# The inverse table of a long convolution: one transposing DMA in place of sixteen TensorE transposes, with a new order of all work

## The chip, the cores and the metric

One Trainium2 chip, of which the kernel uses one core. The metric is the device time in microseconds (us) of one execution. The engines are named as the profile names them: PE (matmuls on TensorE, with PEld its weight loads), ACT (ScalarE), DVE (VectorE), POOL (GpSimd) and SP (the engine that issues most DMAs; DMAs that ACT and POOL issue are named so).

## The reference, cut to what matters

The inputs are 2048 tokens of 640 channels in bf16. The token-wise part is a normalisation and a gated feed-forward network with 1728 hidden units; the sequence part is a causal convolution over all 2048 tokens for each channel, written with FFTs of length 4096.

```python
x = A_q
xn = _layernorm(x, axis=-1)
s = _A_ref(xn, A_k, A_v, A_shift_k, A_ssm_k, A_ssm_D)
g = _silu(_B_ref(xn, B_w1, B_b1, B_w2, B_b2))
return x + s * g
# _A_ref: k_shift = a causal filter of 4 taps over k;  kv = k_shift * v
#         y = irfft(rfft(kv, 4096) * rfft(ssm_k, 4096))[:2048] + kv * ssm_D;  returns xn * y
# _B_ref: h = gelu(x @ w1 + b1);  returns h @ w2 + b2
```

## The kernel before

**Tiles.** The tokens are cut into 16 tiles of 128 rows, tile `i` holding tokens 32k+16h+i (k is 0 to 63, h is 0 or 1). Everything stays in SBUF but the convolution's intermediate results, which pass through three scratch tensors in HBM to be laid out anew.

**The convolution.** The transform is done in two steps on PE. Step 1 multiplies each tile with a table `W` (128 x 16 x 128, one 128 x 128 block for each tile): operations `K1_i`, `K1r_Q` for the filter and `U1_i`, `U1r_Q` for the signal, evicted from PSUM by `Ke`, `Ker`, `Ue`, `Uer` and stored by `Ks_Q`, `Us_Q`. Step 2 loads a slice s of 8 (`KL_s`, `UL_s`) and multiplies with a small table (`K2_s_r`, `U2_s_r`, and `X2_s` for the last 128 channels of both), evicted by `Kf`, `Uf`. The products are `pr_s_w` and `pq_s_w` on DVE. The inverse goes the same way: `i1_s` and `i1r` (evicted by `ie`, `ir`), stores `cs_s`, loads `cl_r`, and `i2_i`, whose weights are `G`, the inverse table. `G` is `W` with each 128 x 128 block transposed, and nothing but `i2` reads it. `ym_i` multiplies the result by the gated and normalised tile, `ad_i` adds x, `os_i` stores.

**The tables.** The angles of `W` are integers made in three groups of tiles (0 to 3, 4 to 9, 10 to 15): `wm` (a multiplication and an addition, on DVE or POOL), `wq` (a mask, on DVE) and `ws` (two sines on ACT).

**The feed-forward part.** `bn_i` takes statistics, `rs_g` (POOL) the reciprocal deviations of a group of tiles, `xn_i` normalises, `xt_i` transposes on PE and `xe_i` evicts. `f1_c_r_ft` is the first matmul for a chunk c of four tiles and 128 hidden units (in two halves r of 256 tokens for chunk 0 and ft below 5, otherwise 512 tokens at once), `ge` its gelu on ACT. `f1h`, `geh` are the last 64 units. `f2_i_h` is the second matmul, 14 products for a half of 320 channels, or 28 of 64 columns each where the order marks it `/N`; `si_i` is the silu on ACT and `gx_i` multiplies on DVE. A change between sine, gelu and silu on ACT loads a table (line 686).

**The shift filter and kv** are the `kv` operations on DVE. `wu_j` are groups of four warm-up matmuls on a zero tile.

**The order.** The functions only declare operations with what they read and write. The string `ORDER` lists all of them, and `Plan.emit` issues them in exactly that order, each on its engine: so every engine's program, and each DMA queue, is a subsequence of `ORDER`. A token `name/E@slots` carries a choice of engine (`A` for ACT, `D` for DVE, `G` for POOL, `S` for SP, `N` for the split matmul; without a letter the first that the operation allows, which is ACT for evictions) and the buffers that it takes from pools: for PE operations a bank of PSUM, of which there are 8 (`@6`, or 6 and 7 for an operation that takes two). A bank can be written again when the operation that evicts it is done. Waits between engines follow from the data.

The inverse table is made in the lines above `w2l`: two PSUM banks are filled with eight transposes each (`gt0`, `gt1`, line 503), and each is copied to `G` by one eviction (`gte0`, `gte1`, line 181, the line of all evictions). In the order before they stand between the first `xt`, and the copies go to DVE.

Of the kernel before, what the change touches and what calls it, by code (L numbers as in the profile page):

```python
# [55 lines left out]
class Plan:  # L56
# [6 lines left out]
    def op(self, name, eng, fn, reads=(), writes=(), hold=(), func=None):  # L63
        o = Op()
        o.name, o.engs, o.fn, o.func = name, eng.split("|"), fn, func
        o.reads, o.writes = list(reads), list(writes)
# [8 lines left out]
        return o
# [39 lines left out]
def h3_block(ctx: ExitStack, tc: tile.TileContext, x_d, k_d, v_d, sk_d, K_d, D_d, w1_d, b1_d, w2_d, out_d):  # L115
    nc = tc.nc
# [63 lines left out]
    def evict(e, out_, in_):  # L180
        (nc.scalar.copy if e == "ACT" else nc.vector.tensor_copy)(out=out_, in_=in_)  # L181

    ps = Pool(8, lambda k, sz: ps_t[:, k:k + 2, :] if sz == 2 else ps_t[:, k, :])
# [310 lines left out]
                out=xn_t[:, i, a:b], in0=xn_t[:, i, a:b], in1=s_.v[:, a:b], op=ALU.mult),  # L494
               reads=[slh[n]], writes=[xnb[i][n]], hold=[s_])

    for g in range(2):
        pb = Buf(pool=ps)

        def gt(e, g=g, pb=pb):  # L500
            o = pb.v.bitcast(BF16).rearrange("p (a b) -> p a b", b=P)
            for t in range(8):
                nc.tensor.transpose(out=o[:, t, :], in_=W_t[:, 8 * g + t, :], identity=ident[:])
# [195 lines left out]
K1_7@6 Ker_1/A f1_0_0_9@4 xl4 Kl0 xn4 Dl/A kl1 f1_0_1_4@5 xn5 Ke_7/A Kl3 xn7 f1_0_0_10@0 xn6 ge_0_0_9 kv0_0@0 Ks_1  # L699
xt5@1.1 ge_0_1_4 f1_0_0_1@2 xe5/A xt4@3 kv0_1m@1 xt7@6 xt6@7 xe7/A f1_0_0_11@4 xe6/A kv0_1a f1_0_0_4@5 xe4/A  # L700
f1_0_1_3@1 ge_0_0_10 f1_1_0_5@6.1 ge_0_0_1 kv0_2m@1 ge_0_0_4 ge_0_1_3 K1_14@2 ge_1_0_5 K1r_3@0 kv0_2a f1h_1@7 Ke_14/A
f1_0_0_12/N@5 Ker_3/A bn12 f1_1_0_9/N@6 ge_0_0_11 Ks_3 bn13 vl0 ge_0_0_12 f1_1_0_8/N@2 w2l1 ge_1_0_9 vl1 kv0_3m@1 w2l0
geh_1 f1h_0@3 ge_1_0_8 K1_8@0.2 K1_10@4 kv0_3a K1_9@6 geh_0 f1_1_0_11@2 Ke_8/A bn14 f1_1_0_0@3 Ke_10/A bn15 f1_1_0_2@0
# [10 lines left out]
kv3_2a U1_15@0.0 U1_14@6 Ue_15/A f2_2_1 kv3_3m@1 Ue_14/A kv3_3a kv3_4 f1_3_0_7@4.0 si_2 bn9 U1_12@0 U1_13@6 Ue_12/A
U1r_3@2 Ue_13/D f1_3_0_4@5 Uer_3/A bn11 K2_2_0@0 K2_3_0@6 Us_3 f1_3_0_5@2 bn10 f1_3_0_12@3 ge_3_0_4 Kf_2_0/D rs3
ge_3_0_7 f1_3_0_0@5 ge_3_0_5 ge_3_0_12 xn8 xn11 K2_7_0@0 ge_3_0_0 xt8@4.0 f1_3_0_9@2 Kf_3_0/A xe8/D xn9 K2_2_1@4 UL0@6
ge_3_0_9 xt11@3 Kf_2_1/D UL1@3 xt9@6 Kf_7_0/A UL2@8 f1_3_0_3@7 UL6@9 xe11/D UL3@10 xe9/D KL6@7 K2_0_1@4 ge_3_0_3
K2_1_1@0 xn10 K2_3_1@2 Kf_0_1/A xt10@6 Kf_3_1/D f1_3_0_1@7 Kf_1_1/A gx_2 K2_7_1@4 xe10/D X2_0@2 ge_3_0_1 gx_5 U2_0_0@0
# [62 lines left out]
```

## Time and profile before

| | |
|---|---|
| median of 3 runs | 183.62 us (183.51 to 183.87) |
| profiled execution, its own time | 184.05 us |
| its span, from first to last instruction | 182.3 us |
| granted TensorE clock | 1.0 |
| busy: PE, DVE, ACT, POOL | 175.0, 160.9, 138.5, 22.6 us |

The profile's views used below: a page with busy times and the costliest groups of instructions (line, engine, operation, result and sources, count, then busy time and mean duration in ns); stretches of the span with the busy time of each engine and the number of its instructions in brackets; the chain of work that ended last (start, duration, engine, result, line, count); and the timeline (start, duration, engine, line, operation, count, and in brackets the idle time before it and what ended it). PEq, SPq and the like are the engines' sequencers, which issue DMAs.

### The profile page before, as it was taken

How to read it: one execution, taken by the hardware profiler on the slowest of the kernel's cores; microseconds unless marked ns; L12 is line 12 of the kernel's file. 1: busy time of each engine (PE TensorE's matmuls, PEld its weight loads, DVE VectorE, ACT ScalarE, POOL GpSimd, SP SyncE). 2: the span in 40 equal slices, each digit the busy share in tenths (PEclk: the TensorE clock that was granted, in tenths of full speed). 3: DMA queues.
4: the chain of work that ended last, by engine and by line, in shares of the span. 5: the costliest groups of instructions: out<-in, count | busy, mean ns of one | idle time of the engine just before them, and what ended most of it. 6: DMA issues, size and time to landing. Idle time of an engine off the chain costs nothing.

```text
span 182.3 us, 5182 instructions
## 1 busy us (share of the span) xinstructions
PE 175.0 (96%) x2192; PEld 99.9 (55%) x2192; DVE 160.9 (88%) x252; ACT 138.5 (76%) x201; POOL 22.6 (12%) x52
## 2 busy tenths in 40 slices
...
GB/s 187 411 415 403 199 367 407 334 425 432 409 309 403 417 358 397 153 287 76 222 340 367 172 141 158 148 325 377 148 4 88 206 287 132 416 405 392 66 189 144
DMA packets 19417, 50.64 MB, mean 278 GB/s; under 512 B 1729, under 2 KB 13506, under 8 KB 17986
## 3 DMA queue, kind: packets, MB, share of 16 engines
...
q8 instruction: 17, 0.28, 0.6%
...
HBM read 31.95 MB, written 18.35 MB: 276 GB/s over the span
## 4 chain that ended last, share of the span: by engine, by line
PE 81%; DVE 8%; ACT 7%; issue 1%; ACTq 0%; DVEq 0%
PE ps L435 30%; PE ps L476 30%; PE ps L349 4%; PE ps L604 4%; PE ps L563 4%; PE ps L413 3%; PE ps L664 2%; DVE xn L668 2%; ACT v L181 2%; DVE stats L381 2%; ACT L686 1%; ACT k L181 1%; PE ps L360 1%; PE ps L450 1%; DVE w L238 1%
## 5 line engine op out<-in xcount | busy, mean ns | idle before, releaser
L476 PE MATMUL ps<-w,hT 128*64 128x320 bf16 (+4 forms) x644 | 65.0, 293 | 0.0
L435 PE MATMUL ps<-xnT,w 128*128 128x512 bf16 (+2 forms) x300 | 61.2, 362 | 0.5 <-ACT sl L489 0.2
L476 PEld LDWEIGHTS <-hT 128*64 128x64 bf16 (+3 forms) x644 | 45.3, 105 | 17.4 <-issue 3.9
L435 PEld LDWEIGHTS <-w 128*128 128x128 bf16 (+1 forms) x300 | 26.4, 99 | 28.5 <-issue 6.2
L181 ACT CAST st<-ps 128x1024 bf16<-128x1024 f32 x36 | 35.0, 1014 | 3.4 <-PE ps L360 1.8
L439 ACT ACTIVATE hT<-ps,b1f 128x512 bf16<-128x512 f32 (+1 forms) x57 | 35.0, 665 | 1.2 <-PE ps L435 1.0
L489 ACT ACTIVATE sl<-ps 128x640 bf16<-128x640 f32 (+2 forms) x18 | 11.6, 647 | 24.0 <-PE ps L476 19.4
L529 DVE TENSOR_TENSOR lat<-lat 128x2560 bf16<-128x2560 bf16 (+1 forms) x15 | 18.4, 1225 | 0.5
L526 DVE TENSOR_TENSOR lat<-k,lat 128x2560 bf16<-128x2560 bf16 (+1 forms) x15 | 18.3, 1218 | 0.2
L181 ACT CAST k<-ps 128x1024 bf16<-128x1024 f32 (+2 forms) x19 | 16.2, 878 | 2.6 <-PE ps L563 1.5
L181 ACT CAST v<-ps 128x1024 bf16<-128x1024 f32 (+2 forms) x18 | 14.5, 839 | 0.4 <-PE ps L563 0.4
L668 DVE TENSOR_TENSOR xn<-ps,xn 128x640 bf16<-128x640 f32 x16 | 12.6, 819 | 2.2 <-PE ps L664 2.0
L493 DVE TENSOR_TENSOR xn<-xn,sl 128x640 bf16<-128x640 bf16 (+2 forms) x18 | 8.0, 448 | 7.3 <-ACT sl L489 7.2
L181 DVE CAST k<-ps 128x1024 bf16<-128x1024 f32 (+2 forms) x14 | 11.8, 857 | 2.3 <-PE ps L563 0.9
L381 DVE BATCH_NORM_STATS2 stats<-x 128x6 f32<-128x320 bf16 x32 | 13.7, 470 | 0.0
L686 ACT ACT_TABLE_LOAD x8 | 10.3, 1283 | 0.1
L396 POOL TENSOR_SCALAR rstd<-mv 128x4 f32<-128x4 f32 (+1 forms) x5 | 1.3, 257 | 69.2 <-DVE mv L382 69.2
L181 ACT CAST lat<-ps 128x1024 bf16<-128x1024 f32 (+2 forms) x12 | 9.4, 826 | 0.2 <-PE ps L604 0.2
L604 PE MATMUL ps<-st,I 32*64 32x512 bf16 x256 | 8.8, 380 | 0.1
L332 PE MATMUL ps<-hT 128*128 128x512 bf16 x24 | 7.5, 477 | 1.2 <-DVE mhalf L212 1.2
L181 DVE CAST lat<-ps 128x1024 bf16<-128x1024 f32 (+2 forms) x9 | 7.9, 892 | 0.7 <-PE ps L604 0.3
L181 ACT COPY xnT<-ps 128x640 bf16<-128x640 bf16 x8 | 5.3, 695 | 3.9 <-PE ps L413 3.9
...
## 6 DMA issues: line engine op xcount, KB each, us to landing
...
v<-in_v SPq DMA_DIRECT2D x4, 640.0 KB, 7.6
k<-scrK SPq DMA_DIRECT2D x4, 640.0 KB, 7.4
v<-scrK SPq DMA_DIRECT2D x4, 640.0 KB, 9.9
w<-in_w SPq DMA_DIRECT2D x2, 1120.0 KB, 10.3
x<-in_x SPq DMA_DIRECT2D x3, 640.0 KB, 6.8
k<-in_k SPq DMA_DIRECT2D x3, 640.0 KB, 7.2
```

The lines of the kernel that those rows point to most:

```text
L181: (nc.scalar.copy if e == "ACT" else nc.vector.tensor_copy)(out=out_, in_=in_)
L381: nc.vector.bn_stats(out=stats[:, i, h, :], in_=x_t[:, i, h * H:(h + 1) * H])
L435: nc.tensor.matmul(out=pb.v[us, 0:b - a], lhsT=w1_t[:, ft, t, us], rhs=xnTb[c].v[:, a // P:b // P, t, :], start=(t == 0), stop=(t == DT - 1))
L439: nc.scalar.activation(out=hTb[c].v[:, ft, a:b], in_=pb.v[:, 0:b - a], func=ACT.Gelu_apprx_tanh, bias=b1_f[:, ft:ft + 1], scale=1.0)
L476: nc.tensor.matmul(out=o[us, 0:b - a], lhsT=hTb[c].v[0:M, ft, q * P + us.start:q * P + us.stop], rhs=w2_t[0:M, ft, a:b], start=(ft == 0), ...
L489: nc.scalar.activation(out=o_, in_=i_, func=ACT.Silu)
L493: op("gx_" + nm, "DVE", lambda e, a=a, b=b: nc.vector.tensor_tensor(out=xn_t[:, i, a:b], in0=xn_t[:, i, a:b], in1=s_.v[:, a:b], op=ALU.mul ...
L526: op("kv%d_%dm" % (r, j), "DVE", lambda e, i=i, n=n, j=j, t=t, wb=wb: nc.vector.tensor_tensor(out=t.v[:, 0:n, :], in0=k_t[:, i + 3 - j:i + ...
L529: op("kv%d_%da" % (r, j), "DVE", lambda e, n=n, t=t, a=a: nc.vector.tensor_tensor(out=a.v[:, 0:n, :], in0=a.v[:, 0:n, :], in1=t.v[:, 0:n, ...
L604: nc.tensor.matmul(out=pb[j // 2].v[64 * a:64 * a + 64, j % 2, :], lhsT=I1_t[32 * j:32 * j + 32, m, :], rhs=o[w][32 * j:32 * j + 32, a, r, ...
L668: op("ym_%d" % i, "DVE", lambda e, i=i, pb=pb: nc.vector.tensor_tensor(out=xn_t[:, i, :], in0=pb.v.rearrange("p a b -> p (a b)")[:, 0:D], ...
L686: nc.scalar.activation(out=tab[:], in_=cst[:], func=func)
```

## The change

The sixteen transposes `gt` and the two evictions `gte` are taken out. One operation `gT` on SP takes their place, a DMA that reads `W` from SBUF and writes `G` in SBUF, transposing each block. It needs all of `W`, and `i2` needs it, as before. All other functions are as they were. The string `ORDER` is replaced as a whole: nearly every operation has another place, many have other PSUM banks, and some go to another engine (`wm0` from DVE to POOL, `sx`, a scaling of a small table, from DVE to POOL, `b1c` from POOL to DVE; 11 of the 16 `xe` on ACT in place of 8, 13 of the 16 `ir` on ACT in place of 9; 14 of the 33 `f2` with `/N` in place of 13). `gT` stands in SP's queue behind the loads `UL0` and `UL1` and ahead of `UL6` and `UL3`; `UL2` goes from SP to POOL.

```diff
-    for g in range(2):
-        pb = Buf(pool=ps)
-
-        def gt(e, g=g, pb=pb):
-            o = pb.v.bitcast(BF16).rearrange("p (a b) -> p a b", b=P)
-            for t in range(8):
-                nc.tensor.transpose(out=o[:, t, :], in_=W_t[:, 8 * g + t, :], identity=ident[:])
-
-        op("gt%d" % g, "PE", gt, reads=Wb + [idb], writes=[pb])
-        op("gte%d" % g, "ACT|DVE", lambda e, g=g, pb=pb: evict(
-            e, G_t[:, 8 * g:8 * g + 8, :], pb.v.bitcast(BF16).rearrange("p (a b) -> p a b", b=P)), reads=[pb], writes=[Gb[g]])
+    op("gT", "SP", lambda e: nc.sync.dma_start_transpose(
+        out=G_t[:], in_=W_t[:].rearrange("p i b -> p (i b)")), reads=Wb, writes=Gb)
...
-b1l/A grid xl1 zz c0 xl0 wu2@0 fix wm0 wm2/G Kl4 w1l0 wm1 xl2 w1l2 wu4@1 wq0 Kl1 wq1 w1l1 sm0 Kl2 wq2 wu0@2 bn2 ws2 id
-skl bn3 ws1 wu5@3 bn1 rs1 w1l3 K1_12@4.0 K1_13@6 K1_15@0 bn0 kl0 Ke_13/A wu3@2 ws0 xn2 wu1@3 rs0 xn3 Ke_12/A xt2@6.0
-gt1@7 b1c xe2/D xt3@2 xn1 gt0@3 xe3/A xn0 xt1@6 sm1 xt0@4 xe1/A f1_0_1_1@5.0 xe0/D sm2 f1_0_1_0@2 bn4 f1_0_0_7@6
-gte0/D ge_0_1_1 f1_0_0_8@4 bn5 ge_0_1_0 ge_0_0_7 Ke_15/A f1_0_1_2@5 bn7 f1_0_0_5@3 ge_0_1_2 gte1/D ge_0_0_8 one1 bn6
-K1_4@0.2 ge_0_0_5 K1_5@6 f1_0_0_0@2 Ke_4/A Ke_5/D rs2 f1_0_0_6@5 ge_0_0_0 sm3 K1_6@0 ge_0_0_6 K1r_1@2 one0 Ke_6/D
...
-pr_7_1@1 i1r_3@0.4 Uf_5_1/A f2_11_1 ir_6_0/A pr_5_0@3 ir_7_0/A ir_7_1/D i1_7@2.0 ir_6_1/D si_11 pr_5_1@2 cs_6/S
-f1_3_0_10@4 ie_7_1/A ie_7_0/D i1_5@6.0 cs_7/S f2_10_0@2.1 ie_5_0/A ie_5_1/D gx_11 cs_5/S f2_10_1 f1h_3@5 si_10
-f2_8_1/N@6.0 cl_0@8 gx_10 cl_2@6 cl_1/G@10 cl_5/G@4 f2_8_0/N cl_7/G@7 cl_3/G@0 f2_9_0/N@0.1 cl_6/G@1 si_8 gx_8 i2_1@2
-i2_0@6 ge_3_0_10 ym_1 f2_9_1/N geh_3 ad_1 ym_0 i2_5@2 ad_0 i2_4@4 ym_5 f2_14_1/N@6.0 si_9 os_0 os_1 ym_4 cl_4@2 ad_4
-i2_3@0 gx_9 os_4 i2_2@2 ym_3 i2_10@4 f2_14_0/N ym_10 ym_2 i2_11@0 ad_2 si_14 i2_14@4 ym_11 f2_12_1/N@2.1 os_2 ym_14
...
+b1l/A grid xl1 zz xl0 wu5@0 fix wm1 wm2/G w1l0 Kl4 w1l1 wq1 xl2 wu1@1 c0 ws1 w1l2 Kl2 id wq2 w1l3 bn3 wm0/G ws2 wu2@2
+skl bn2 kl0 wu3@3 bn0 rs1 wu4@4 bn1 Kl3 K1_13@6.0 K1_15@0 xn2 Ke_13/A K1_12@2 rs0 xn3 xt2@5.0 xt3@4 xe2/D Ke_15/A
+wu0@6 sm0 xn1 xn0 xe3/A xt1@7 wq0 xt0@5 b1c/D f1_0_1_0@6.0 xe1/D xe0/A Ke_12/D f1_0_1_4@0 ws0 f1_0_1_2@1 sm1
+f1_0_0_8@4 bn5 sm2 f1_0_0_6@7 ge_0_1_0 bn7 ge_0_1_4 f1_0_0_4@5 ge_0_0_6 bn4 f1_0_0_3@2 ge_0_0_4 f1_0_0_5@3 ge_0_1_2
+bn6 ge_0_0_3 ge_0_0_8 K1r_1@6.2 ge_0_0_5 K1_7@0 K1_4@4 rs2 f1_0_0_7@2 Ker_1/D Ke_4/A K1_6@4 ge_0_0_7 one0 K1_5@6 xn4
...
+Kf_3_0/A f1_3_0_7@4 ge_3_0_0 xn8 f1_3_0_4@5 ge_3_0_7 xn11 xn10 xn9 UL0@3 K2_3_1@0 ge_3_0_4 K2_1_1@2 UL1@8 UL2/G@9
+K2_2_0@6 Kf_1_1/A gT f1_3_0_1@4 Kf_2_0/D sx Kf_3_1/A xt8@5.1 xt9@2 xe8/D xt11@3 ge_3_0_1 K2_2_1@6 xe11/D K2_0_1@0
...
+Kf_7_2/D Uf_7_2/D f2_11_0@2.1 ie_4_1/A pq_7_1 pq_7_0 ie_4_0/A pr_7_1@2 i1r_3@0.6 cs_4/S pr_7_0@0 U2_5_1@4 ir_7_1/A
+f2_11_1 ir_6_0/A ir_6_1/A Uf_5_1/D ir_7_0/A cs_6/S pr_5_0@1 i1_7@6.0 si_11 pr_5_1@3 f1_3_0_10@4 ie_7_0/A gx_11
+ie_7_1/A i1_5@2.6 gx_4 cs_7/S f2_8_0@0.1 ie_5_0/D ie_5_1/A cs_5/S f1h_3@5 f2_8_1/N geh_3 f2_10_0/N@6.0 si_8 cl_0@9
+cl_2@8 cl_5/G@7 gx_8 cl_1/G@4 f2_10_1/N cl_6/G@6 cl_7/G@0 f2_9_0/N@2.1 si_10 cl_3/G@1 gx_10 i2_0@0 i2_1@6 ge_3_0_10
+ym_0 f2_9_1/N ym_1 ad_0 ad_1 i2_5@4 si_9 i2_4@0 ym_5 f2_14_1/N@6.0 ad_5 ym_4 os_5 os_1 i2_10@2 ad_4 cl_4@3 i2_3@4 gx_9
+i2_2@0 os_4/A f2_14_0/N ym_2 ym_10 ym_3 i2_11@0 si_14 f2_12_1/N@2.1 ad_3 ad_2 os_3/A ym_11 ad_10 i2_12@4 i2_14@6 ym_12
...
```

More of the change, by code (lines that the diff above doesn't have):

```diff
@@ L699 @@
[L699 to L703, printed above, removed]
@@ L714 @@
[L714 to L718, printed above, removed]
@@ new lines @@
+ge_0_0_0 f1h_1@1.1 ge_0_0_9 f1h_0@0 kv0_2m@1 geh_1 f1_1_0_2/N@6 geh_0 kv0_2a f1_1_0_8/N@7 ge_1_0_2 ge_0_0_1 K1_14@2
+K1_10@0.2 kv0_3m@1 Ke_14/A K1r_3@4 f1_1_0_5@6 Ker_3/A bn12 f1_0_0_11@2 Ke_10/A Ks_3 bn14 vl1 f1_0_0_2@3 ge_1_0_5 w2l1
+f1_1_0_10@4 w2l0 bn15 ge_0_0_2 ge_0_0_11 f1_1_0_4@5 kv0_3a ge_1_0_10 ge_1_0_8 K1r_2@0 ge_1_0_4 K1_1@2.0 K1_9@6 kv0_4
+f1_0_1_3@4 Ker_2/A f1_1_0_0@5 Ke_9/A bn13 f1_1_0_7@0 ge_1_0_0 kv1_1m@1 ge_0_1_3 f1_1_0_1@1 Ke_1/A kv1_0@0 ge_1_0_7
+K1_11@6 K1_8@4 ge_1_0_1 K1_2@2 f1_1_0_3@0 Ke_11/A Da rs4 Ke_2/D f1_1_0_12@1 Ke_8/A one1 kv1_1a ge_1_0_3 Ks_2 K1_3@6
@@ new lines @@
+K1_0@2 kl2 Ke_3/A K1r_0@4 f1_1_0_9@0 xn12 Ker_0/A xn13 kv1_2m@1 f1_1_0_11@6 ge_1_0_9 ge_1_0_12 f1_1_0_6@7 kv1_2a
+f2_3_1@4.0 ge_1_0_6 xn14 Ke_0/A kv1_3m@1 ge_1_0_11 Ks_0 f2_3_0 vl2 kv1_3a kl3 vl3 xt14@0.0 si_3 kv1_4 f2_6_0@2.1
+xe14/A sm3 xn15 kv2_0@1 U1_2@6.2 U1r_0@4 U1_0@0 f2_6_1 Ue_0/A kv2_1m@0 Ue_2/A KL7@0 KL0@1 xt13@0 Uer_0/A kv2_1a xt15@1
+xe13/A si_6 kv2_2m@0 xe15/A kv2_2a gx_3 f2_1_1@6.0 U1_3@4 U1_1@2 U1_7@0.0 Ue_1/A f2_1_0 Ue_7/A kv2_3m@0 Ue_3/A xt12@2
+si_1 Us_0 KL1@4 kv2_3a xe12/A KL3@2 kv2_4 gx_6 f2_0_0@0.1 U1_4@4 U1r_1@6 U1_6@2 Uer_1/A f2_0_1 Ue_4/A kv4_1m@0 Ue_6/A
@@ new lines @@
+kv4_0@1 si_0 kv4_1a kv4_2m@0 gx_1 f2_7_0@6.0 U1_10@4.2 U1_5@2 U1_11@0 Ue_5/A f2_7_1 kv4_2a ss Us_1 kv4_3m@0 xl3
+Ue_11/A KL2@5 kv4_3a Ue_10/A kv4_4 si_7 gx_0 f2_5_1@2.1 U1_9@0 U1_8@4 kv3_0@0 Ue_9/A U1r_2@6 f2_5_0 kv3_1m@1 Uer_2/A
+kv3_1a Ue_8/A kv3_2m@1 K2_0_0@0 K2_1_0@6 si_5 Us_2 kv3_2a Kf_0_0/A kv3_3m@1 Kf_1_0/A kv3_3a kv3_4 gx_7 f2_2_0@4.0
+U1_15@2.0 U1_14@0 Ue_15/A f2_2_1 Ue_14/A bn10 U1_13@6 si_2 U1_12@2 U1r_3@0 Ue_12/D Ue_13/A f1_3_0_12@4.0 Uer_3/A bn9
+f1_3_0_5@5 Us_3 gx_2 f1_3_0_9@6 KL6@6 bn8 ge_3_0_12 K2_3_0@2 bn11 K2_7_0@0 ge_3_0_5 f1_3_0_0@7 ge_3_0_9 Kf_7_0/D rs3
@@ new lines @@
+Kf_3_0/A f1_3_0_7@4 ge_3_0_0 xn8 f1_3_0_4@5 ge_3_0_7 xn11 xn10 xn9 UL0@3 K2_3_1@0 ge_3_0_4 K2_1_1@2 UL1@8 UL2/G@9
+K2_2_0@6 Kf_1_1/A gT f1_3_0_1@4 Kf_2_0/D sx Kf_3_1/A xt8@5.1 xt9@2 xe8/D xt11@3 ge_3_0_1 K2_2_1@6 xe11/D K2_0_1@0
+xe9/A xt10@5 f1_3_0_3@4 Kf_0_1/A xe10/D Kf_2_1/D K2_7_1@2 ge_3_0_3 X2_0@0 Kf_7_1/A U2_0_0@6 f2_4_0@4.0 Uf_0_2/A
+Uf_0_0/A Kf_0_2/D pq_0_0@2 U2_1_0@2 U2_0_1@0 Uf_1_0/A f2_4_1 UL6@10 Uf_0_1/D UL3@7 pr_0_1@3 U2_1_1@6 si_4 U2_2_0@2
+X2_1@0 pr_0_0@0 Uf_1_1/A f1_2_0_6@4.1 pq_0_1 Uf_1_2/D UL4@1 f1_2_0_11@5 Kf_1_2/D ge_2_0_6 Uf_2_0/D i1_0@6.0 ge_2_0_11
@@ new lines @@
+pq_1_1 f1_2_0_3@4 ie_0_0/A pq_1_0 pr_1_0@1 ie_0_1/A i1r_0@2.6 f1h_2@5 ir_1_0/D ir_0_1/A ir_1_1/A pr_1_1@0 X2_6@0
+ir_0_0/A ge_2_0_3 U2_2_1@6 U2_6_0@2 Kf_6_2/A Uf_2_1/D KL4@4 f1_2_0_0@4 Uf_6_2/A cs_0/S geh_2 Uf_6_0/D i1_1@0.6
+ge_2_0_0 f1_2_0_10@5 ie_1_0/D ie_1_1/A X2_2@2 pr_2_1@2 ge_2_0_10 U2_6_1@6 Kf_2_2/A U2_3_0@0 f1_2_0_9@4 Uf_6_1/D
+Uf_2_2/A Uf_3_0/A X2_3@2 pr_2_0@3 KL5@3 ge_2_0_9 U2_3_1@6 X2_4@0 Uf_3_2/A pq_2_0@0 f1_2_0_2@5 Kf_4_2/A Kf_3_2/D
+Uf_3_1/A pq_3_1 f1_3_0_6@4 pq_2_1 ge_2_0_2 pq_3_0 Uf_4_2/D UL5/G@5 i1r_1@2.6 ge_3_0_6 pr_3_0@1 K2_6_0@0 ir_3_0/A
```

40 lines of the change are left out of this document (12 added, 28 removed).

## The prediction

> **What bounds the kernel now.** I read the page's first part, then the stretches of the span, then the chain of work, and last the timeline where the two orders differ.
>
> ```profile
> PE 175.0 (96%) x2192; PEld 99.9 (55%) x2192; DVE 160.9 (88%) x252; ACT 138.5 (76%) x201; POOL 22.6 (12%) x52
> ```
>
> PE is the bound overall. Stage by stage, in columns PE, PEld, DVE, ACT, POOL with instruction counts, then granted clock and DMA:
>
> ```profile
> 12.10:30.00 17.90, 17.90 (x150) 10.68 (x149) 17.09 (x30) 16.81 (x28) 5.76 (x16) 1.00 0.93 341
> 95.00:137.00 42.00, 41.42 (x843) 19.32 (x829) 39.92 (x55) 40.26 (x62) 4.07 (x5) 1.00 0.62 206
> 137.00:156.00 19.00, 18.61 (x263) 12.25 (x259) 9.80 (x13) 10.68 (x16) 2.67 (x5) 1.00 0.59 194
> 156.00:166.00 10.00, 9.33 (x134) 7.08 (x136) 8.70 (x14) 4.31 (x8) 0.00 (x0) 1.00 1.02 410
> 166.00:178.70 12.70, 12.59 (x214) 10.17 (x208) 12.46 (x26) 2.21 (x5) 0.00 (x0) 1.00 0.51 185
> ```
>
> From its first real matmul at 12.1 us on, PE hardly waits: 0.58 us of 42 in the middle, 0.39 before the tail, 0.67 and 0.11 in the tail. So a new order of the same matmuls can win about 1.7 us there at most, while ACT and DVE at 95% in the middle say how easily it loses some. The rest is the start, which the chain shows:
>
> ```profile
> 9.65 0.32 DVE xn L403
> 10.02 0.45 PE ps L413 x5
> 10.47 0.45 PE ps L503 x8
> 10.92 0.28 PE ps L413 x5
> 11.20 0.45 PE ps L503 x8
> 11.64 0.65 PE ps L413 x10
> 12.29 4.88 PE ps L435 x30
> ```
>
> Both groups of eight transposes (line 503) lie on the chain, 0.45 us each, ahead of the first matmul of the network at 12.29.
>
> **The change part by part.**
>
> *Removed: 0.90 us of PE, two evictions of DVE.*
>
> ```profile
> L181 DVE COPY G<-ps 128x1024 bf16<-128x1024 bf16 x2 | 1.3, 638 | 0.0
> L439 ACT ACTIVATE hT<-ps,b1f 128x512 bf16<-128x512 f32 x47 | 31.1, 702 | 1.2 <-PE ps L435 1.0
> L439 ACT ACTIVATE hT<-ps,b1f 128x256 bf16<-128x256 f32 x10 | 4.5, 492 | 0.0
> L243 ACT ACTIVATE W<-w,cst 128x256 bf16<-128x256 int32 x2 | 1.0, 564 | 0.0
> L181 ACT CAST k<-ps 128x256 bf16<-128x256 f32 x3 | 1.1, 387 | 0.0
> L181 ACT COPY xnT<-ps 128x640 bf16<-128x640 bf16 x8 | 5.3, 695 | 3.9 <-PE ps L413 3.9
> L181 ACT CAST st<-ps 128x1024 bf16<-128x1024 f32 x36 | 35.0, 1014 | 3.4 <-PE ps L360 1.8 <-PE ps L349 1.5
> ```
>
> DVE loses its two evictions, 1.28 us, behind the first matmuls of the network, where it is not the bound (PE is busy all of 17.90). Whether PE gains its 0.90 depends on what else holds the first `f1`.
>
> *The start.* The new order runs xt2, xt3, four warm-up matmuls (`wu0`), xt1, xt0, f1.
>
> ```profile
> 2.67 1.79 POOL L234 TENSOR_SCALAR w<-w 128x384 int32<-128x384 int32 x1
> 5.56 0.87 DVE L381 BATCH_NORM_STATS2 stats<-x 128x6 f32<-128x320 bf16 x2
> 7.77 1.90 PE L332 MATMUL ps<-hT 128*128 128x512 bf16 x8
> 10.12 0.77 POOL L397 TENSOR_TENSOR rstd<-rstd,mhalf 128x2 f32<-128x2 f32 x1
> 10.99 0.80 DVE L403 TENSOR_SCALAR xn<-x,mv,rstd 128x640 bf16<-128x640 bf16 x2
> 12.68 1.28 ACT L686 ACT_TABLE_LOAD   x1
> 14.09 1.40 ACT L439 ACTIVATE hT<-ps,b1f 128x256 bf16<-128x256 f32 x3
> ```
>
> Eight warm-up matmuls take 1.90, so wu0 takes 0.95: it fills on PE just what the transposes leave. What shortens is DVE: wm0 goes to POOL, and wq0 behind xn0. But wq2 now stands directly ahead of the statistics and waits for POOL's wm2, which ends at 2.67 + 1.79 = 4.46; with 0.85 for wq2 (row below) the statistics start at 5.31, not 5.56. Everything behind moves by that 0.25 to 0.35: rs0 on POOL, then xn1 and xn0 (10.99 + 0.80 = 11.79 becomes 11.45), then xt0 at 0.28: the first f1 at about 11.85 instead of 12.29. **Term 1: -0.4.** Bounds: -0.9 if the 0.90 falls off the chain in full, 0 if POOL (wm0 now sits between wm2 and rs1) is later.
>
> ```profile
> L238 DVE TENSOR_SCALAR w<-w 128x768 int32<-128x768 int32 x2 | 1.6, 848 | 0.0
> ```
>
> *ACT after the start.* ws0, two sines of 564 ns, had run before the xe; now it stands behind xe0, and the gelu table load behind it. xe0 can start at 11.85 and ends at 12.55; ws0 ends at 13.7; load 1.28 and its dummy activation bring the first gelu to 15.1, against 14.09. PE fills PSUM meanwhile: K1_4 takes banks 4 and 5, and bank 4 is free after the seventh gelu (five of 492 and two of 702, 3.9 us): 19.0. PE gets there after five narrow and three wide f1 (three of each take 4.88 in the chain, so 0.55 and 1.08), K1r_1 and K1_7 (0.5): 11.85 + 2.75 + 3.24 + 0.5 = 18.35. A wait of about 0.6; where gelus run back to back they overlap a little (three narrow in 1.40), which leaves 0.2. **Term 2: +0.4**, bounds 0 (ACT catches up before the bank is asked for) and +1.0 (the gelus' whole delay).
>
> *The middle.* Counted from X2_0 to i1_5 in both orders and priced by the groups' means, PE has the same 45.7 us, DVE falls from 50.2 to 48.4 (four small evictions `ir`, and `sx`), ACT rises from 48.8 to 49.7 (the four `ir`, less one gelu). PE idled 0.58 there. **Term 3: -0.3**, bounds -0.6 (no idle time left) and +0.9 (all of ACT's addition shows).
>
> *gT.* It reads and writes 0.5 MB, in SP's queue behind UL0 and UL1.
>
> ```profile
> 90.65 1.92 SPq L550 DMA_DIRECT2D lat<-scrU  x3
> 107.61 0.44 PE L563 MATMUL ps<-lat,F 64*32 64x512 bf16 x8
> ```
> ```profile
> lat<-scrU SPq DMA_DIRECT2D x3, 640.0 KB, 9.2
> k<-in_k SPq DMA_DIRECT2D x1, 1120.0 KB, 13.8
> ```
>
> No transposing DMA is in this trace. The nearest rows: a 640 KB load from scratch lands in 9.2 us, the longest load in 13.8. What it holds up is UL6, issued at about 91 and first used at 107.6: 16.6 - 9.2 = 7.4 us of slack. Its own result is used 60 us later. From below it costs 0; if it held SP for the whole 13.8, UL6 would be 6.4 late. I take 0: a transfer of 0.5 MB is nearer to the 640 KB row, a sequencer is normally free again within a microsecond (three issues in 1.92), and DMA is busy 62% in that stage. UL2's move to POOL has the same cover.
>
> [...]
>
> *The hand-over to the tail.* The tail starts when cs_5 has landed and cl_0 has come back:
>
> ```profile
> 139.52 0.57 PE ps L632 x32
> 142.10 1.00 PE ps L604 x32
> 156.04 0.48 PE ps L664 x4
> ```
> ```profile
> 141.17 1.28 ACT L686 ACT_TABLE_LOAD   x1
> 146.76 0.36 SPq L644 DMA_DIRECT2D scrC<-k  x1
> 151.62 0.33 SPq L656 DMA_DIRECT2D lat<-scrC  x1
> ```
>
> i1r_3 ends at 140.09, ACT starts its silu load 1.08 later, and cs_5 goes out at 146.76, 10.7 us of stores, loads and cover before the first i2. In the new order ACT has four ir first (4 x 0.39 = 1.6), then the load, si_11 (0.7) and both ie_7, and i1_5 needs bank 6, which ie_7_0 frees: load at 1.6, si_11 from 3.1, ie_7_0 (1.0) done at 4.8, where PE, with U2_5_1, a half of f2 (2.0), i1_7 (1.0) and one f1 (1.08) ahead of it, could have started i1_5 at about 4.5. **Term 4: +0.3**, bounds 0 and +0.6. PE's cover ahead of the first i2 is 10.2 us, as before, and one more split f2 (0.11 shorter) lies in it and buys nothing.
>
> *The tail.*
>
> ```profile
> 162.31 0.46 PE L664 MATMUL ps<-v,G 128*64 128x512 bf16 x4 [0.63 <-DVE xn L668]
> 162.81 1.56 DVE L668 TENSOR_TENSOR xn<-ps,xn 128x640 bf16<-128x640 f32 x2 [0.53 <-PE ps L664]
> ```
>
> PE waited 0.63 for a bank that a ym had not read yet, then DVE 0.53 for PE. In the new order f2_14_1 stands ahead of i2_10, i2_3 and i2_2, so the bank of i2_2 is asked for about 5.6 us after the first i2, and ym_4 has read it at about 4.9. Both engines have the same work from there. **Term 5: -0.5**, bounds -0.7 and +0.3 (DVE has two more operations behind the last f2 than before, and it was idle only 0.2 at the end).
>
> *Sum.* -0.4 + 0.4 - 0.3 + 0 + 0.3 - 0.5 = -0.5, against the profiled execution's 184.05 (1.75 around its span of 182.3): 183.55. The median of the runs, 183.62, is 0.43 below that execution, so 183.1.
>
> **The rivals.**
>
> *ACT becomes the bound (slower).* Over all, ACT takes on 2.7 us (three xe of 0.69, four ir, less two others) while DVE drops 4.5. For it: ACT is busy 16.81 of 17.9 in the first stage and 40.26 of 42 in the middle. Place: the first gelus, a microsecond late. It decides once PSUM's 8 banks can't hold that microsecond, and the lag then stays up to the first f2, since ACT had 1.1 us idle in 17.9 to recover. Price: term 2 at +1.0, term 3 at +0.6, term 4 at +0.6, terms 1 and 5 half: 183.6 + 1.75 = 185.4 at most, 184.5 as its middle.
>
> *The transposes were hidden anyway (no change).* The first f1 is set by POOL and DVE (rs0, xn0), and wu0 fills PE; what terms 3 and 5 give, 2 and 4 take: 183.6.
>
> *gT holds SP's queue.* Decides from 7.4 us on; at 13.8 it costs 6.4: about 189.5. [...]
>
> **How the numbers follow.** Two runs differ by up to 0.2% in the times shown, 0.37 us; less than that counts as no change. Forecast (faster, about 183.1, own range 182.0 to 183.25): 0.44. No change: 0.19. ACT-bound: 0.33, of which a few hundredths reach past 185. gT: 0.04. The low end: term 1 at -0.9, terms 3 and 5 at their bounds with the rest as taken is -1.5, so 182.1. The high end leaves out gT and the worst of ACT: 184.9.
>
> **What would show it.** Right: the first L435 matmul near 11.85; no L503; PE idle under 0.4 us in the middle; no wait of an L664 for DVE in the tail; UL6's matmuls not waiting for a DMA. Wrong: PE waiting for ACT between 18 and 21 us; an ACT more than 97% busy from 95 to 137; cs_5 issued more than 6.7 us after i1r_3; SP silent for over 7 us behind the transposing DMA.

## The result and the profile after

The kernel after takes 182.25 us (median of 10 runs, 181.9 to 183.09), the kernel before 183.69 beside it (10 runs). The ratio is 0.9917, 95% interval 0.9895 to 0.9939: 1.44 us faster. The profiled execution of after took 183.09 us, with a span of 181.3. Its busy times:

```profile
PE 173.2 (96%) x2185; PEld 102.8 (57%) x2185; DVE 157.3 (87%) x242; ACT 143.5 (79%) x211; POOL 26.5 (15%) x54
```

Line numbers behind line 497 (`gT`) are 9 lower than before. The start and the hand-over in the timeline of after, PE's rows first, then SP's (columns: start, duration, engine, line, operation, and in brackets the idle time before it and what ended it):

```profile
8.79 0.82 PE L349 MATMUL ps<-xn,W 64*128 64x512 bf16 x6 [1.17 <-DMA xn<-in_ssm_k]
...
11.15 0.72 PE L413 MATMUL ps<-ident,xn 128*128 128x128 bf16 x10
11.80 6.13 PE L435 MATMUL ps<-xnT,w 128*128 128x256 bf16 x40
17.86 0.40 PE L360 MATMUL ps<-x,W 64*128 64x128 bf16 x8
...
155.25 0.73 PE L655 MATMUL ps<-lat,G 128*64 128x512 bf16 x8 [0.69 <-DMA lat<-scrC]
```
```profile
145.57 0.36 SPq L635 DMA_DIRECT2D scrC<-v  x1
149.55 0.83 SPq L647 DMA_DIRECT2D lat<-scrC  x2
```

The first f1 is at 11.80 (12.13 in the timeline of before; the chain, which counts from the release, had 12.29), the table's transposes are gone, and PE does not wait between 12 and 30 us. The last scratch store (cs_5) goes out at 145.57 instead of 146.76, and cl_0, which waits for it, 3.98 us later instead of 4.86. The stretches, with the columns of the prediction's table:

```profile
12.00:30.00 18.00, 18.00 (x153) 10.78 (x153) 17.15 (x31) 17.69 (x32) 5.41 (x16) 1.00 0.98 374
95.00:137.00 42.00, 41.27 (x801) 19.44 (x800) 38.87 (x52) 40.72 (x63) 3.07 (x4) 1.00 0.65 198
```

The transposing DMA in SP's queue, and its time to landing:

```profile
89.43 0.50 SPq L541 DMA_DIRECT2D lat<-scrU  x1
89.97 6.97 SPq L497 DMA_TRANSPOSE G<-W  x1
97.00 1.39 SPq L541 DMA_DIRECT2D lat<-scrU  x1
```
```profile
G<-W SPq DMA_TRANSPOSE x1, 10.4
```

It holds SP for 6.97 us. UL6 goes out at 97.00, lands 5.4 us later and is used at 106.2: nobody waits.

At the end the tail has a new wait. ACT's rows in the timeline of after:

```profile
175.12 0.44 ACT L489 ACTIVATE sl<-ps 128x320 bf16<-128x320 f32 x1 [1.74 <-DVE x L663]
175.14 1.52 ACTq L642 DMA_DIRECT2D out<-x  x2
176.71 0.60 ACT L489 ACTIVATE sl<-ps 128x160 bf16<-128x160 f32 x2 [1.16 <-DVE x L663]
```

The two stores are os_0 and os_8. ACT's queue holds os_8 until ad_8 (line 663) is done on DVE, and si_15_1 stands behind it. PE's last matmul ends at 176.98 and the span at 181.3, 4.3 us behind it; before, it was 3.7.

Stage by stage, each row counted from the end of the one above it (before, after; us): start to first f1 12.13, 11.80; to the first f2 35.85, 35.42; to K2_0_0 28.60, 28.39; to X2_0 18.51, 18.24; to the end of i1r_3 45.00, 44.85; to the end of i1_5 5.23, 5.55 (U2_5_1 now lies in it); to the first i2 10.72, 11.00; to PE's end 22.55, 21.73; to the end of the span 3.7, 4.3.

### The profile page after: what moved, and what is told of

It reads as the page before. It is cut to its first block, busy times and chain, and to the rows that moved or that the text cites. A ratio compares the mean times of both kernels' runs of the same rounds, so it can differ in the third digit from the quotient of the medians.

```text
span 181.3 us, 5164 instructions
## 1 busy us (share of the span) xinstructions
PE 173.2 (96%) x2185; PEld 102.8 (57%) x2185; DVE 157.3 (87%) x242; ACT 143.5 (79%) x211; POOL 26.5 (15%) x54
## 4 chain that ended last, share of the span: by engine, by line
PE 68%; DVE 11%; DMA 9%; ACT 8%; issue 1%; SPq 1%; ACTq 0%; DVEq 0%
PE ps L435 29%; PE ps L476 19%; DVE xn L659 6%; PE ps L595 5%; PE ps L349 5%; PE ps L554 4%; DMA xn<-in_ssm_k 4%; DMA lat<-scrC 3%; ACT v L181 3%; PE ps L413 3%; DVE x L663 2%; ACT k L181 2%; DMA scrC<-v 2%; ACT hT L439 1%; DVE xn L493 1%
## 5 line engine op out<-in xcount | busy, mean ns | idle before, releaser
L476 PEld LDWEIGHTS <-hT 128*64 128x64 bf16 (+3 forms) x658 | 47.9, 105 | 14.9 <-issue 3.8
L181 ACT CAST st<-ps 128x1024 bf16<-128x1024 f32 x35 | 33.7, 1020 | 7.8 <-PE ps L349 5.1
L181 ACT CAST k<-ps 128x1024 bf16<-128x1024 f32 (+2 forms) x23 | 19.1, 867 | 1.2 <-PE ps L623 0.6
L181 ACT CAST v<-ps 128x1024 bf16<-128x1024 f32 (+2 forms) x18 | 14.1, 806 | 0.3 <-PE ps L595 0.3
L396 POOL TENSOR_SCALAR rstd<-mv 128x4 f32<-128x4 f32 (+1 forms) x5 | 2.3, 455 | 64.0 <-DVE mv L382 64.0
L181 DVE CAST k<-ps 128x512 bf16<-128x512 f32 (+2 forms) x10 | 8.1, 819 | 2.5 <-ACT k L181 1.6
L181 DVE CAST lat<-ps 128x1024 bf16<-128x1024 f32 (+2 forms) x9 | 9.6, 1072 | 0.6 <-PE ps L595 0.5
L181 DVE CAST v<-ps 128x1024 bf16<-128x1024 f32 (+2 forms) x8 | 8.4, 1054 | 1.8 <-PE ps L595 0.7
L579 DVE TENSOR_TENSOR st<-lat,v 128x512 bf16<-128x512 bf16 (+1 forms) x12 | 9.6, 819 | 0.0
```

Source lines behind the costliest of these rows:

```text
L476: nc.tensor.matmul(out=o[us, 0:b - a], lhsT=hTb[c].v[0:M, ft, q * P + us.start:q * P + us.stop], rhs=w2_t[0:M, ft, a:b], start=(ft == 0), ...
```

## The experiments

Three questions. What does the DMA give, and what the order? What in the order wins the stretch from the first f1 to the end of i1_5, where PE had no waits to lose? And why do the scratch's landings differ? Ratios are to the kernel before, on the same chip.

**The DMA in the old order.**

```diff
-gt1@7 gt0@3 gte0/D gte1/D
+KL6@7 gT
```

> Edit: in the order of before, gt0, gt1, gte0 and gte1 go out and the transposing DMA goes in behind KL6's load, where SP then has nothing to issue for 15 us; everything else keeps the order of before. Theory A (the transposes are a small part of the gain, most of it is the new order): in the order of before the first f1 needs xn0's transposes anyway, so it starts 0.2 to 0.4 us earlier, at 11.9 to 12.1 us, PE keeps this to the end, and the ratio to the kernel before is near 0.998 (0.2 to 0.4 us). Rival B (the transposes were the whole gain): 1.4 us, ratio 0.992. Rival C (they were hidden): ratio 1.000 and first f1 at 12.29.

Measured: 182.67 us against 183.41, ratio 0.9955 (0.9933 to 0.9977), 0.74 us. Rival C was right that the first f1 does not move; no theory had the gain where it lies. The start, in PE's rows of this run:

```profile
10.02 0.81 PE L413 MATMUL ps<-ident,xn 128*128 128x128 bf16 x10 [0.35 <-DVE xn L403]
11.48 0.81 PE L413 MATMUL ps<-ident,xn 128*128 128x128 bf16 x10 [0.66 <-DVE xn L403]
12.13 1.04 PE L435 MATMUL ps<-xnT,w 128*128 128x256 bf16 x8
```

Where the transposes had been, PE now waits 0.66 us for xn, and the first f1 is at 12.13, as before. In the old order the transposes cost nothing there. Every step up to the end of i1_5 stands within 0.01 us of before (145.32 in both). The gain is all behind it: first i2 at 155.46 instead of 156.04, and PE's wait of 0.63 us in the tail gone (21.70 instead of 22.55 us from the first i2 to PE's end). cl_0 went out 3.89 us after cs_5, not 4.86:

```profile
146.74 0.36 SPq L635 DMA_DIRECT2D scrC<-k  x1
150.63 0.33 SPq L647 DMA_DIRECT2D lat<-scrC  x1
```

**The new order with the PE transposes.**

```diff
-Kf_1_1/A gT f1_3_0_1@4
+f1_0_0_4@5 gt0@0 ge_0_0_6 gte0/D bn4 f1_0_0_3@2 gt1@6 ge_0_0_4 gte1/D
```

> Edit: the order of after, with the sixteen PE transposes and their two evictions on DVE in place of the transposing DMA. gt0 stands behind f1_0_0_4 and gt1 behind f1_0_0_3, where PE has no wait. Theory A (the new order carries most of the gain, PE is the bound in this stage): PE gets 0.90 us more of its own work there and everything behind it is 0.9 us later than in after, so the ratio to the kernel before is near 0.997 (1.44 less 0.9, a gain of 0.5 us). Rival B (the DMA carries the whole gain): no gain, 1.000. Rival C (PE has room there, the transposes cost nothing): as after, 0.992.

Measured: 183.73 us, ratio 1.0012 (0.9989 to 1.0034), no gain. PE's rows:

```profile
15.85 0.61 PE L503 MATMUL ps<-ident,W 128*128 128x128 bf16 x8
16.30 0.71 PE L435 MATMUL ps<-xnT,w 128*128 128x256 bf16 x5
16.84 0.61 PE L503 MATMUL ps<-ident,W 128*128 128x128 bf16 x8
17.29 1.24 PE L435 MATMUL ps<-xnT,w 128*128 128x512 bf16 x5
18.90 0.40 PE L360 MATMUL ps<-x,W 64*128 64x128 bf16 x8 [0.37 <-DVE G L181]
```

From the first f1 to the first f2 it took 36.81 us against 35.42: 1.39 more, of which 0.90 is the transposes and 0.37 a wait for their eviction's bank. The number is rival B's, but the reason is theory A's at a higher price: the transposes cost nothing at the start, where PE waits for xn anyway, and 1.39 us where PE is the bound. What the new order wins besides was used up by them, and in this execution by 0.6 us more in the tail, where PE waited for a load of the scratch. They can't stand earlier in the order as it is: they read all of `W`, and `ws0` stands behind `xe0` in it. A new order with `ws0` ahead and the transposes in place of `wu0`, where PE waits for xn, was not run, so it is open whether the new order needs the DMA.

**Four more switches.**

```diff
-U1_0@0 f2_6_1   U1_7@0.0 f2_1_0   U1_6@2 Uer_1/A f2_0_1   U1_11@0 Ue_5/A f2_7_1
+f2_6_1 U1_0@0   f2_1_0 U1_7@4.0   Uer_1/A f2_0_1 U1_6@2   Ue_5/A f2_7_1 U1_11@0
```

> Edit: the order of after; in the stage of the first f2 tiles four blocks of K1/U1 matmuls are cut in two: U1_0, U1_7, U1_6 and U1_11 move behind the f2 half that followed them, with the evictions turned so that no bank is waited for. The same matmuls run on PE, but PE goes four times more from full-array matmuls (128 rows) to split ones (64 rows) and back. Theory A (each such round trip costs PE about 0.21 us: 0.10 by the first U1 pair of a block, 0.32 against 0.22 us, and 0.11 by the first f2 half behind it, 2.01 against 1.90): K2_0_0 starts 0.85 us later than in after, at 76.5 instead of 75.68, without a wait on PE, and the time is 183.1 us (ratio to the kernel before 0.9965). Rival B (the switches are free, the order gained by waits on ACT and DVE): K2_0_0 at 75.7 and the ratio of after, 0.992.

Measured: 183.44 us, ratio 0.9989 (0.997 to 1.0009). The first f2 was at 46.94 and K2_0_0 at 76.67: 29.73 us, against 28.39 in after, 1.34 more for the same matmuls. Split means here a matmul on 64 or 32 rows of the array (64*128, 64*32 and 32*64 in the rows), not the `/N` of an f2, which keeps 128. PE's rows where one of the four blocks was cut in two, first of after, then of this run:

```profile
58.55 0.82 PE L349 MATMUL ps<-v,W 64*128 64x512 bf16 x6
59.30 2.08 PE L476 MATMUL ps<-w,hT 128*128 128x320 bf16 x14
61.22 0.44 PE L413 MATMUL ps<-ident,xn 128*128 128x128 bf16 x5
```
```profile
58.47 1.04 PE L349 MATMUL ps<-v,W 64*128 64x512 bf16 x4
59.44 2.08 PE L476 MATMUL ps<-w,hT 128*128 128x320 bf16 x14
61.52 0.39 PE L349 MATMUL ps<-v,W 64*128 64x512 bf16 x2
61.85 0.45 PE L413 MATMUL ps<-ident,xn 128*128 128x128 bf16 x5
```

Four matmuls took 1.04 here and 0.61 in every other block of this stage: 0.43 is a wait that my order added. The other 0.91 is four round trips between full matmuls and split ones, with a second, short wait in the block shown; the three other blocks, which have no wait, grew by 0.19, 0.21 and 0.21. So a round trip cost about 0.2 us here, as expected. It is the cost that the prediction lacked. Counted in `ORDER` from the first f1 on, PE makes 40 such trips before and 37 after: one fewer in each of the three stages up to X2_0, and the same number behind it. That stands against gains of 0.43, 0.21 and 0.27 in these stages. The first of these holds something more: in both executions of before PE starts an f1 about 0.17 us late there for a gelu, a wait too short for the views to list. The 0.15 gained up to i1r_3 and the 0.32 lost behind it are no trips: U2_5_1, 0.34 us of work, went from the one stage to the other.

**gT one place earlier on SP.**

```diff
-UL1@8 UL2/G@9 K2_2_0@6 Kf_1_1/A gT
+gT UL1@8 UL2/G@9 K2_2_0@6 Kf_1_1/A
```

> Edit: the order of after with the transposing DMA one place earlier on SP, between UL0 and UL1. Theory A (SP is held for the whole 6.97 us and what stands behind waits): UL1 is issued near 96.4 instead of 89.4 us, lands 5.6 us later at 102, U2_1_0, which ran at 96.7, waits for it, and the kernel is about 5 us slower than after (187 to 188 us). Rival B (the hold is only the issue of a long transfer and the next load's data flows beside it): UL1 still lands before 97 us and the time stays at 182.3 us.

Measured: 192.94 us, 10.7 over after (one run). Both theories missed. SP's rows and PE's, then the landing of UL1:

```profile
89.11 3.86 SPq L497 DMA_TRANSPOSE G<-W  x1
93.03 1.20 SPq L541 DMA_DIRECT2D lat<-scrU  x2
...
105.10 0.63 PE L554 MATMUL ps<-lat,F 64*32 64x512 bf16 x8 [8.64 <-DMA lat<-scrU]
```
```profile
lat<-scrU SPq DMA_DIRECT2D x1, 640.0 KB, 12.0
```

SP was held for only 3.86 us, but the 640 KB load behind the transposing DMA landed 12.0 us after its issue, not 5.6 as in after, and PE stood still for 8.64. The two loads behind that one landed after 13.2 and 14.1 us, against 9.8 and 10.9 where no transposing DMA stands ahead of them (the run with gT late, below). The price of the transposing DMA was paid in this run by the loads behind it, by the first of them with 6.4 us, more than the 3.86 us for which SP was held.

The wait itself explains 8.64 of the 10.7 us. Most of the rest goes with the granted clock: 3.8 us into the wait it fell to 0.50, and it came back only 5.4 us after PE had begun again (stretches of this run, in the columns of the prediction's table):

```profile
105.00:109.00 4.00, 3.90 (x28) 1.81 (x29) 2.67 (x3) 2.50 (x3) 0.00 (x0) 0.50 0.39 133
111.00:112.00 1.00, 1.00 (x13) 0.50 (x6) 0.82 (x2) 0.98 (x2) 0.00 (x0) 1.00 0.39 59
```

**Before, once more.** No edit.

> Edit: none, the kernel before, for a second profiled execution. With the DMA alone (the run with the old order) every step up to the end of the last inverse transform, 145.32 us, stood where it stood in the profile of before to 0.01 us; its whole gain lay behind it: the last scratch store landed after 3.89 us instead of 4.86, the first i2 came 0.58 us earlier and the i2 stage was 0.85 us shorter, because two waits of PE for loads of the scratch were gone. Theory A (the landing of that store and of the loads varies from one execution to the next): a second execution of before has the first i2 anywhere between 155.46 and 156.3, and if it is 155.46 its span is near 181.0. Rival B (the transposing DMA changes these landings in every execution): a second execution of before has the waits again: store landing over 4.7 us, first i2 near 156.0, span near 182.3.

Measured: 183.21 us, span 181.3. The store took 4.87 us to release cl_0 again, and the first i2 was at 155.93, so the late landing belongs to the kernel. The wait in the tail did not come again (21.73 us from the first i2 to PE's end), so it was of one execution. The store's and the load's issue in this one:

```profile
146.81 0.36 SPq L644 DMA_DIRECT2D scrC<-k  x1
151.68 0.33 SPq L656 DMA_DIRECT2D lat<-scrC  x1
```

**After, once more.** No edit.

> Edit: none, the kernel after, for a second profiled execution and for its time beside the two runs that follow on the same chip. From the four runs before: first f1 at 11.5 or 11.8, from there to the end of i1_5 132.45 us in every execution (132.46, against 133.81 with the four switches), so i1_5 ends at 143.96 or 144.25. PE has 10.13 us of its own from there to the first i2. Theory A (the wait for the first load of the scratch varies): first i2 between 154.1 (no wait) and 155.3. Rival B (the new order leaves less cover, so it waits in every execution): first i2 at 155.0 or later again. Ratio to the kernel before 0.992 by both.

Measured: 182.29 us, ratio 0.9938 (0.9917 to 0.9959). From the first f1 (12.00) to the end of i1_5 it took 132.46 us, as in the first (132.45). The first i2 was at 154.59, without a wait, so the 0.69 us of the first profile is of one execution. Between them the two profiles of after give a span 0.75 us shorter than the two of before: start -0.24, first f1 to i1_5 -0.75, to the first i2 -0.08, to PE's end -0.42, and behind PE's end +0.74. The medians differ by more, 1.44 and 1.09 us: both profiled executions of after (183.09 and 182.57) are slower than their medians, so a part of the gain, some 0.3 to 0.7 us, is in no profile and its place is not shown.

**The scratch loads on SP.**

```diff
-cl_5/G@7 cl_1/G@4 cl_6/G@6 cl_7/G@0 cl_3/G@1
+cl_5@7   cl_1@4   cl_6@6   cl_7@0   cl_3@1
```

> Edit: the order of after with the five scratch loads that POOL issues (cl_5, cl_1, cl_6, cl_7, cl_3) on SP, behind cl_0 and cl_2 in the order of use. Theory A (in after cl_0 landed 5.6 us after its issue, against 4.2 with the DMA alone, because POOL's five loads began beside it only 0.8 us after it; on one queue they come behind it): cl_0 lands 4.0 to 4.4 us after its issue, the wait of 0.69 us ahead of the first i2 goes, the time is 0.6 us less than after (ratio to the kernel before 0.9885). Rival B (one queue moves the loads too slowly, or the stores of the result queue up behind them): a later load is waited for, time equal to after or up to 2 us more.

Measured: 182.67 us, ratio 0.9959 (0.9944 to 0.9974): slower than after, if anything. The first i2 came without a wait, as in the second execution of after, and no load was waited for. But the first f1 was at 11.52 in this execution, 0.48 earlier than in that one, and the span is the same 180.8: 4.9 us pass behind PE's last matmul, against 4.5. ACT waited there 1.24 us for a store of the result, where the second execution of after waited 1.3.

**Two stores off ACT.**

```diff
-os_5 os_1        ...   ym_9 os_12        ...   ad_8        ...   si_15_0 os_0/A gx_15_0 os_8/A   ...   si_15_2 os_7
+os_5 os_1 os_0   ...   ym_9 os_7 os_12   ...   ad_8 os_8   ...   si_15_0 gx_15_0               ...   si_15_2
```

> Edit: the order of after with the stores os_0 and os_8 issued by SP instead of ACT, os_0 behind os_1 and os_8 behind ad_8, and os_7 one place earlier on SP. Theory A (in after ACT's queue holds os_8, which waits for ad_8 on DVE, ahead of si_15_1, and the end of the program comes 4.3 us after PE's last matmul instead of 3.7): the 1.16 us wait of ACT goes and the end is 0.6 us earlier, ratio to the kernel before 0.9885. Rival B (the last store's landing sets the end, ACT's wait is covered): no change, ratio 0.992.

On SP os_7 moved by three stores, ahead of os_12, os_10 and os_9, not by one; which of the three moves counts was not tried apart. Measured: 181.47 us, ratio 0.9897 (0.9875 to 0.992), 0.82 below after on the same chip. ACT's rows:

```profile
174.59 0.44 ACT L489 ACTIVATE sl<-ps 128x320 bf16<-128x320 f32 x1 [1.74 <-DVE x L663]
175.51 0.30 ACT L489 ACTIVATE sl<-ps 128x160 bf16<-128x160 f32 x1 [0.49 <-PE ps L476]
176.48 0.30 ACT L489 ACTIVATE sl<-ps 128x160 bf16<-128x160 f32 x1 [0.67 <-PE ps L476]
```

The silus of the last two parts follow PE again, and the span ends 3.9 us behind PE's last matmul. This version is faster than both kernels.

**Both at once.** The kernel before, with the transposing DMA added and nothing taken out; it writes `G` a second time with the same values.

```diff
+KL6@7 gT
```

> Edit: the kernel before with its PE transposes and their evictions kept, and the transposing DMA added behind KL6's load; it writes the same values over G once more. In two executions of before the last scratch store landed 4.86 and 4.87 us after its issue (cl_0 then follows); in seven with the transposing DMA, old order or new, 3.88 to 3.98 us. Theory A (the added DMA, or what it does to the queue behind it, makes that store land sooner): landing 3.9 us, first i2 at 155.46, a ratio to the kernel before of 0.9955 as with the DMA alone, although nothing is taken off PE. Rival B (taking the transposes off PE does it): landing 4.87 us and the ratio of no change, 1.000.

Measured: 183.87 us, ratio 1.0038 (1.0018 to 1.0059), slower. cl_0 went out 5.46 us after cs_5. So it is not the added DMA that makes the store land sooner. What goes with the landing is seen in the DMA view of the 3.3 us from the store's issue on. Its queue lines for before, then for this run, then for the DMA in the old order (columns: packets, MB, share of the engines' time):

```profile
q1 hardware_dynamic: 779, 0.96, 85.7%
q8 instruction: 1, 0.02, 1.8%
q14 instruction: 1, 0.01, 0.6%
```
```profile
q1 hardware_dynamic: 899, 1.11, 96.5%
q8 instruction: 1, 0.02, 1.8%
```
```profile
q1 hardware_dynamic: 918, 1.14, 97.9%
```

In before (both executions) and here a 16 KB packet of the queue "instruction" runs inside the store, 1.2 to 1.9 us after its issue, for about 1 us on one of the 16 DMA engines (1.8% of their 3.3 us is 0.95 us of one), and it looks as if one engine then goes on alone when the others are done: in before the last 19 packets of the store come one at a time from 150.12 to 151.06, and from 150.1 to 151.6 the 16 engines are busy 4.2%. In the kernels without the PE transposes that packet comes 3.3 to 3.5 us after the store's issue, at its very end, and cl_0 goes out after 3.88 to 4.00 us (ten profiles); in the new order with the PE transposes it comes after 3.7, with 4.35. With the packet inside: 4.86, 4.87, 5.46. The kernels differ there by the instructions of the transposes, so the packet's time may follow from the count of instructions ahead of it, which no run shows. That it is the cause of the late landing is read from these records; no run moved the packet alone. This run lost 0.5 us more between 104 and 140 us and 0.35 at the start, which I did not follow up.

**gT late.** On the version with two stores off ACT:

```diff
-Kf_1_1/A gT f1_3_0_1@4   ...   UL7@2 ge_3_0_8
+Kf_1_1/A f1_3_0_1@4      ...   UL7@2 gT ge_3_0_8
```

> Edit: the order of after with the two stores on SP (the run before this one in that respect), and the transposing DMA moved behind UL7's load, where SP has nothing to issue for 19 us. Theory A (what holds SP and delays the landing is the traffic beside it: in after it held SP for 6.97 us and landed after 10.4, between two other loads it held SP for 3.86 and made loads behind it land after 12 to 14 us instead of 4 to 6): it holds SP for less than 5 us and lands in less than 8, and the time stays that of the stores' run, ratio 0.990. Rival B (the hold is the transfer's own): 6.5 to 7 us of hold and 10 us to landing again, ratio 0.990 as well because nothing waits there. If the place of the DMA ahead of the scratch stores matters to their landing, the landing of the last store is not 3.9 us any more and the first i2 comes later by the difference.

Measured: 181.62 us, ratio 0.9909 (0.9884 to 0.9934), the time of the stores' run. gT held SP for 5.23 us and landed after 9.3:

```profile
119.26 5.23 SPq L497 DMA_TRANSPOSE G<-W  x1
```

With only UL7's load ahead of it in SP's queue it is still 9.3 against 10.4; theory A missed both its bounds. Two scratch stores that POOL issues ran beside it, so no run shows the transfer quite alone. Hold and landing had no fixed relation over the runs: 5.23 and 9.3 us here, 6.97 and 10.4 in after, 3.86 and 14.3 in the run with gT one place earlier. The store's landing, 3.98 us, is that of after, so the DMA's other place did not change it.

**The two stores, once more.** No edit.

> Edit: none against the run with the two stores on SP; a second execution of it, for its time. Theory A: ratio 0.990 again and an end 3.8 to 3.9 us behind PE's last matmul. Rival B (the gain was chance): the ratio of after, 0.992 to 0.994, and 4.3 us.

Measured: 181.59 us, ratio 0.9904 (0.9882 to 0.9926), 3.9 us behind PE's last matmul: the gain stands.

**Without wu0.** On the same version, with the four matmuls on zeros left out:

```diff
-xe2/D Ke_15/A wu0@6 sm0 xn1
+xe2/D Ke_15/A sm0 xn1
```

> Edit: the run with the two stores on SP, without wu0, the block of four matmuls on zeros that the new order has between xt3 and xt1 (it computes nothing that is used). In six executions of the new order the first f1 was at 11.51 three times (K1_13 did not wait for its load) and at 11.80 to 12.00 three times (it waited 1.17 or 1.72 us for the load, up to 9.0 us, and the rest follows it). Theory A (xt1 waits for xn1 and xn0 from DVE, wu0 lies beside that): first f1 at 11.5 to 11.7, no change in time that can be measured (ratio 0.990). Rival B (wu0 is on the path): first f1 at 10.9 to 11.2 and 0.6 us less.

Measured: 181.63 us, ratio 0.9906 (0.9885 to 0.9927), no difference. The first f1 is at 11.83, with K1_13 at 8.83 behind its load. In wu0's place PE waits for xn:

```profile
11.03 0.80 PE L413 MATMUL ps<-ident,xn 128*128 128x128 bf16 x10 [0.72 <-DVE xn L403]
```

## Why the prediction was right, and where it was wrong

The sign was right, and 182.25 lies in the range of 182.1 to 184.9, near its low end. The forecast of 183.1 is 0.85 too high. Over the two pairs of profiles its terms 1 to 5 measure -0.24, 0, +0.17, -0.08 and +0.32 us, together +0.17 in place of -0.5; the gain is 0.92 in the stretch from the first f1 to X2_0, to which the sum gave no gain at all. So the sign was right by luck, as far as the profiles show: the step that failed is the one that took PE's busy time as fixed. Of the signs listed, PE's idle time in the middle (0.73, not under 0.4) was missed, and one of the wrong ones came: cs_5 went out 6.87 us behind i1r_3's end, over the 6.7 given.

- **Term 1, the start (-0.4).** Size about right: -0.33 in the first pair of profiles, -0.24 over two pairs, -0.1 to -0.6 in single executions. The step that wu0 "fills on PE just what the transposes leave" is true but idle: with neither transposes nor wu0 PE waits for xn (0.66 in the first run, 0.72 in the last). The gain is DVE's and POOL's earlier xn0, which belongs to the order; so the rival "the transposes were hidden anyway" was right on the DMA's share of the start. What then spreads it is a load that I had not considered: K1_13 waits for the filter's load up to 8.6 to 9.0 us in most executions of the new order, and where it does not, the first f1 is at 11.5. That load used up part of what the statistics gave: they started at 4.63, not 5.31, because wm2 ended at 4.04 and not 4.46 and wq2 took 0.64 us and not 0.85.
- **Term 2, ACT (+0.4).** The wait did not come. The first gelu was late as worked out (14.91 for 15.1), but PE was busy 18.00 of 18.00: the term's lower bound of 0. I had priced the seven gelus ahead of bank 4 by group means, 3.9 us; five narrow and two wide ones, which one row shows together, ran in 3.24, because five of the six behind the first started 0.10 to 0.13 us before the one ahead of them ended:

```profile
14.91 3.24 ACT L439 ACTIVATE hT<-ps,b1f 128x256 bf16<-128x256 f32 x7
```

Bank 4 was free at 18.15, and PE asked for it at 18.31. The rival "ACT becomes the bound" falls with it, but in the middle it was not without cost: PE waited 0.28 us there for an eviction on ACT, which it did not in before.

```profile
113.20 0.41 PE L554 MATMUL ps<-v,F 64*32 64x512 bf16 x8 [0.28 <-ACT v L181]
```

- **Term 3, the middle (-0.3).** Not as given. The term counted from X2_0 to i1_5, and there it is +0.17: -0.15 up to the end of i1r_3 and +0.32 behind it. PE idles 0.73 us in the middle by the stretches, against 0.58 before.
- **The missing term.** That PE hardly waits, and so "a new order of the same matmuls can win about 1.7 us there at most", treated PE's busy time as fixed. It is not: switches between full and split matmuls count as busy, 0.19 to 0.21 us a round trip in the run with four more of them, and from the first f1 to X2_0 the order saves three of them, some 0.6 us. That stretch is 0.91 shorter, and the sum had 0 for it, apart from term 2.
- **gT (0).** Right, closer than argued. I took a sequencer to be free within a microsecond; it was held for 6.97, and UL6 went out at 97.00, 7 us later than in the run with gT late (89.74). It landed only 2.8 us later (102.40 for 99.57), with 3.8 us to spare: 5.4 us to landing in place of 9.8, UL0 and UL1 having landed by its issue (at 93.2 and 95.0). The rival on SP's queue was real one place further up. The 13.8 us of hold that this rival was priced with came in no run: SP was held for 3.86 to 9.72. The sixteen blocks landed in 9.3 to 10.7 us in seven profiles (14.3 in the run with gT one place earlier); the 640 KB load just ahead of gT in after landed in 5.6 us and these 512 KB in 10.4, so gT took longer than that load.
- **Term 4, hand-over (+0.3).** i1_5 did not wait for ie_7_0, which was done 4.44 us behind i1r_3's end and not 4.8: ACT's chain is too long by the same overlap as in term 2. i1_5 started at 4.46, the 4.5 that PE alone needs. PE's own work up to the first i2 stayed 10.1 us. What decides is the landing of cs_5 and cl_0, which I took as given: 4.86 before, 3.98 after, and in the first profile of after 5.6 for cl_0. So the +0.28 of the first pair comes near the term by luck.
- **Term 5, tail (-0.5).** Wait for ym gone, as forecast, though that wait of before did not come again in its second execution: against that one the tail gains nothing up to PE's end (21.73 and 21.71). The +0.3 bound, "DVE has two more operations behind the last f2", hit: about 0.7, and not by DVE's time but by os_8 on ACT's queue behind one of them.
